# A background pump's credit in a four-layer attention kernel: income 0.6 and cap 1.0 changed to 0.56 and 0.6

## The chip, the cores and the metric

One core of one Trainium2 chip runs the whole program. The metric is the device time of one execution in microseconds. A set of runs is given by its median, and two kernels are compared by the ratio of their mean times in the same rounds on the same chip, with a 95% interval. Faster or slower needs 2%.

## The reference

Four attention layers in a row on x (2048 rows of 640), each with a layer norm before and a residual after, 32 heads of 20. Layers 0 and 2 (weights A) look back over a window of 256 keys; layers 1 and 3 (weights B) look at all 2048.

```python
x = x + _A_ref(_layernorm(x), A_wqkv, A_wo)   # windowed, W = 256
x = x + _B_ref(_layernorm(x), B_wqkv, B_wo)   # full
x = x + _A_ref(_layernorm(x), A_wqkv, A_wo)
x = x + _B_ref(_layernorm(x), B_wqkv, B_wo)
# each: qkv = x @ wqkv; p = softmax(mask(q k^T * 20**-0.5)); (p v) @ wo
```

## The kernel before

The kernel is recorded as one stream of **tiles**. A tile is three PSUM banks of scores (two, in every second tile of layer 0 and of the start of layer 1), one exponential on ScalarE over all of them, and later the products with v. Between the scores of one tile and those of the next, the recording loop puts **background work**: projections of q, k and v (groups of five matmuls into one bank, which VectorE then empties), output projections (groups of eight), transposes, and the small matmuls of a unit's "tail" (the division by the softmax sum). Each task is a generator. `pump` lets tasks run as long as there is credit; `choose` picks the task; a matmul of 512 columns costs 0.22, one of 320 columns 0.14.

```python
    def choose(blocked, limit=1 << 30):
        if state["held"] is not None:
            return state["held"]
        for t in tails:
            if t.wake <= state["tick"]:
                return t
        if not blocked:
            for t in todo:
                if t.wake <= state["tick"] and (t.need <= limit or t.holds):
                    return t
        return None

    def pump(credit):
        state["credit"] = min(state["credit"] + credit, 1.0)
        while True:
            t = choose(state["credit"] <= 0.0)
            if t is None:
                break
            state["credit"] -= advance(t)
```

```python
    def project(wt, n, xt, dst):
        mb = yield from take_m()
        pq = ps[:, mb, :]
        for dc in range(KD):
            nc.tensor.matmul(
                pq, lhsT=wt[:, n, dc, :], rhs=xt[:, dc, :],
                start=(dc == 0), stop=(dc == KD - 1),
            )
            if dc < KD - 1:
                yield ("hold", 0.22)
        evac(dst(), pq)
        drop_m(mb)
        yield ("pe", 0.22)
```

A full layer's unit (one head group, one chunk of 512 queries) starts only when its projections are stored in device memory and read back. `require` forces missing tasks out at once, whatever the credit; `load_ahead` issues the loads of the next units as soon as what they need is recorded.

```python
    def require(what):
        n = 0
        while what not in ready:
            n += 1
            assert n < 100000, what
            t = choose(False, state["unit"] if n < 400 else 1 << 30)
            if t is None:
                state["tick"] += 1
                continue
            state["credit"] = max(state["credit"] - advance(t), -1.0)
# ...
    def load_ahead():

        for u in full:
            if id(u) not in loaded:
                ensure_loaded(u, False)
                return
```

The loop, cut:

```python
        for t in range(len(tiles) + 8):
            # ... start_unit(u) for units that begin here: require(...) and the loads
                sp = ps[:, 0:3, :] if t % 2 == 0 else ps[:, 3:6, :]
                for n in range(2):
                    for i, (u, j, m, b0, subs, first, last, end) in enumerate(cur):
                        for kc, q0, qn, col in subs[n : n + 1]:
                            nc.tensor.matmul(
                                sp[:, i, col * P : (col + qn) * P],
                                lhsT=u.k(kc, j), rhs=u.q(j, q0, qn), start=True, stop=True,
                            )
            # ... the exponential into pt (L804)
                load_ahead()
                pump(1.2 if cur[0][0].l == 0 else 0.6)
            else:
                pump(2.0)
            # ... masks, and the products with v of the tile two or three before (L843)
```

From layer 1's second part on, one single bank (number 6) serves all background work.

The softmax here doesn't subtract the row's maximum and nothing guards it: scores larger than these inputs give would overflow.

Of the kernel before, what the change touches and what calls it, by code (L numbers as in the profile page):

```python
# [31 lines left out]
def kernel(  # L32
# [119 lines left out]
    state = {"tick": 0, "held": None, "credit": 0.0, "early": True, "act": True, "unit": 0}  # L152
# [15 lines left out]
    def push(name, gen, need):  # L168
        insort(todo, Task(name, gen, need))
# [7 lines left out]
    def advance(task):  # L177
        state["running"] = task
        try:
            kind, n = next(task.gen)  # L180
        except StopIteration:
            drop(task)
            state["held"] = None
            return 0.0
        state["held"] = task if kind == "hold" else None
        if kind == "wait":
            task.wake = state["tick"] + n
            return 0.0
        return n
# [10 lines that stand above are left out]
                    return t  # L200
        return None

    def pump(credit):
        state["credit"] = min(state["credit"] + credit, 1.0)
        while True:
            t = choose(state["credit"] <= 0.0)
            if t is None:
                break
            state["credit"] -= advance(t)
# [23 lines left out]
# [10 lines that stand above are left out]
# [261 lines left out]
    def push_layer(l, c):  # L504

        need = [first_use(l, c, g) for g in range(G)]
        push(("ln", l, c), t_ln(l, c), need[0])
        if l == 1:
            push(("v", l, c, 0), t_v(l, c, (0,)), need[0])
            push(("v", l, c, 1), t_v(l, c, (1,)), need[4])  # L510
        else:
            push(("v", l, c), t_v(l, c, (0, 1)), need[0])
        for g in range(G):
            key = ("qk", l, c, g)
            if l % 2:
                push_proj(key, l, 1, g, t_qk_full(key, l, c, g), need[g])
            else:
                push_proj(
                    key, l, 0, g, t_qk_window(key, l, c, g), need[g], first=(l == 0 and c == 0)
                )  # L520
# [206 lines left out]
    def t_stats0(c):  # L727
        for i in range(4):
            stats(0, c, i)
            yield ("pe", 0.1)  # L730
        ready.add(("x", 0, c))
# [12 lines left out]
    with tc.manual_schedule():  # L744
        push("stats", t_stats0(0), 0)
        push_layer(0, 0)
        require(("xnT", 0, 0))
        other_constants()
        require(("qk", 0, 0, 0))

        def narrow(u):
            return u.l == 0 or (u.l, u.part) == (1, "a")

        banks = [b for u in units for b in u.banks]
        tiles = []
        n = 0
        while n < len(banks):
            size = 2 if len(tiles) % 2 and narrow(banks[n][0]) else 3
            tiles.append(banks[n : n + size])
            n += size  # L760

        started = set()
        pts = deque()
        pushed = set()
        for t in range(len(tiles) + 8):
            state["tick"] += 1
            n_b = 0
            if t < len(tiles):
                cur = tiles[t]
                n_b = len(cur)  # L770
                for b in cur:
                    u = b[0]
                    if id(u) not in started:
                        started.add(id(u))
                        if u.l == 0 and u.g == 0 and u.c + 1 < NC and u.c not in pushed:
                            pushed.add(u.c)
                            push(("stats", u.c + 1), t_stats0(u.c + 1), index[0, u.c + 1, 0, None])
                            push_layer(0, u.c + 1)
                            if u.c == 0:
                                push("prep_b", t_prep_b(), index[0, 1, G - 1, None])  # L780
                        state["unit"] = index[u.l, u.c, u.g, u.part]
                        state["act"] = u.l == 0
                        if state["early"] and not narrow(u):
                            end_early()
                        start_unit(u)
# [8 lines that stand above are left out]
                for b in cur:  # L794
                    if b[-1]:
                        s_emitted(b[0])
                pt = ptp.tile([P, 3, C], BF16, name="pt", tag="pt")
                i = 0
                while i < n_b:
                    b0 = cur[i][3]  # L800
                    k = i
                    while k < n_b and cur[k][3] == b0:
                        k += 1
                    nc.scalar.activation(  # L804
                        out=pt[:, i:k, b0 * P :], in_=sp[:, i:k, b0 * P :],
                        func=ACT.Exp, scale=SCALE,
                    )
                    i = k
                for i, b in enumerate(cur):
                    pts.append((t, pt, i, b))  # L810
                load_ahead()
                pump(1.2 if cur[0][0].l == 0 else 0.6)
            else:
                pump(2.0)

            if 0 < t <= len(tiles):
                cur_, pt_ = masked
                i = 0
                while i < len(cur_):
                    m, b0 = cur_[i][2:4]  # L820
                    k = i
                    while k < len(cur_) and cur_[k][2] == m:
                        k += 1
                    if m is not None:
                        mv_ = masks[:, m, b0 * P :].unsqueeze(1).to_broadcast(
                            (P, k - i, C - b0 * P)
                        )
                        nc.vector.tensor_tensor(  # L828
                            out=pt_[:, i:k, b0 * P :], in0=pt_[:, i:k, b0 * P :], in1=mv_,
                            op=ALU.mult,  # L830
                        )
                    i = k
            if n_b:
                masked = (cur, pt)

            if len(pts) >= 4 and pts[3][0] <= t - (3 if pts[0][3][0].windowed else 2):
                group = [pts.popleft() for _ in range(4)]
                u, subs, end = group[0][3][0], group[0][3][4], group[3][3][7]
                first, last = group[0][3][5:7]
                for n, (kc, q0, qn, col) in enumerate(subs):  # L840
                    for _, pt, i, b in group:
                        j = b[1]
                        nc.tensor.matmul(  # L843
                            op[32 * j : 32 * j + VW, q0 * P : (q0 + qn) * P],
                            lhsT=u.v(kc, j), rhs=pt[:, i, col * P : (col + qn) * P],
                            start=(first and n == 0), stop=(last and n == len(subs) - 1),
                            skip_group_check=u.windowed,
                        )
                if end:
                    pv_emitted(u)  # L850
                    finish_unit(u)
        while tails or todo:
            state["tick"] += 1
            pump(5.0)


# [28 lines left out]
```

## Time and profile before

| | before |
|---|---|
| time, four runs of the first comparison | 2526.7 us median (2521.3 to 2529.6) |
| span of the profiled run | 2512.9 us |
| ScalarE (ACT) busy | 2264.0 us, 90% |
| ACT's waits for score matmuls, 376 to 1760 us | 114.1 us in 113 waits |
| the same from 1760 us on | 5.1 us in 7 waits |

In the page's strip of 40 slices each digit is the busy share in tenths; in a group line "busy, mean ns" is followed by the engine's idle time just before these instructions and by what ended it; in a wait line stand the total, the number and the longest. The lines themselves stand in the prediction. The profiled execution is a fast one: it was timed at 2514.7 us, below all four of the first comparison, so the trace of an ordinary execution looks some 7 us or more worse against it than the times are. What is to be learnt from the lines is that ACT is the bound, and that only the stage of layers 1, 2 and the start of 3 still has idle time on it worth winning.

### The profile page before, as it was taken

Reading aid. Unit: us, or ns where it says so; the run is one execution under the profiler, and the core shown is the slowest. Engines: PE = TensorE matmul, PEld = TensorE weight load, DVE = VectorE, ACT = ScalarE, POOL = GpSimd, SP = SyncE. Lnnn points to the kernel's source line nnn. Section 1 sums busy time; section 2 is a strip of 40 time slices with the busy share of each in tenths; the row PEclk is TensorE's granted clock in tenths of the full one; section 3 lists DMA queues with packets and bytes.
Section 4 is the critical chain, followed back from the end, with each engine's and each line's share of the span. In section 5 each row is a group of like instructions: output and inputs, shape, how many; then the busy total and the mean of one; then the engine's idle time right before and its main releaser. Section 6 shows DMA issues by size and latency. Waiting matters only on the chain.

```text
span 2512.9 us, 37403 instructions
## 1 busy us (share of the span) xinstructions
PE 2049.3 (82%) x15313; PEld 730.0 (29%) x15424; DVE 851.9 (34%) x1925; ACT 2264.0 (90%) x1831; POOL 48.2 (2%) x113
## 2 busy tenths in 40 slices
PE   6788987887878898778987888888877787778777
PEld 3334432222322233223332233223322222222222
DVE  6787842321324333434343433643300010001001
ACT  6778866899998999899999988899999999999995
POOL 2000000000000000000000000000000000000000
PEclk9999998885866689757896589869755565556555
DMA  4212133332210133011221023204211010011100
GB/s 162 72 59 64 51 107 91 111 107 68 67 45 26 34 95 110 30 32 41 90 93 39 8 75 104 66 14 122 79 36 48 32 43 32 33 46 46 32 17 11
DMA packets 92892, 153.03 MB, mean 61 GB/s; under 512 B 8880, under 2 KB 59056, under 8 KB 92720
## 3 DMA queue, kind: packets, MB, share of 16 engines
q1 hardware_dynamic: 92720, 150.64, 19.4%
q8 instruction: 120, 1.97, 0.3%
q14 instruction: 52, 0.43, 0.1%
HBM read 120.46 MB, written 30.15 MB: 60 GB/s over the span
## 4 chain that ended last, share of the span: by engine, by line
ACT 47%; PE 28%; issue 13%; DVE 9%; DMA 2%; SPq 0%; ACTq 0%; POOL 0%; DVEq 0%
ACT pt L804 46%; PE ps L318 9%; PE ps L790 6%; PE ps L843 4%; PE ps L482 4%; PE ps L405 4%; DVE pt L828 3%; DMA wqk<-wqk_d 1%; DVE oT L668 1%; PE ps L369 1%; DVE st L266 1%; DMA qt<-q_d 1%; DVE on L718 1%; DVE qa L266 1%; DVE x_sb L490 1%
## 5 line engine op out<-in xcount | busy, mean ns | idle before, releaser
L804 ACT ACTIVATE pt<-ps 128x1536 bf16<-128x1536 f32 (+1 forms) x1688 | 2198.2, 1537 | 184.6 <-PE ps L790 167.3
L790 PE MATMUL ps<-qt,kt 32*128 32x512 bf16 x4096 | 713.9, 504 | 302.4 <-ACT pt L804 268.8
L843 PE MATMUL ps<-pt,vt 128*21 128x512 bf16 x4096 | 533.8, 507 | 6.0 <-DVE oT L668 3.6
L790 PEld LDWEIGHTS <-kt 32*128 32x128 bf16 x4096 | 204.2, 95 | 771.5 <-issue 738.3
L318 PE MATMUL ps<-xnT,wqk 128*128 128x512 bf16 x1169 | 345.0, 413 | 34.8 <-DMA wqk<-wqk_d 7.8
L828 DVE TENSOR_TENSOR pt<-pt,masks 128x1024 bf16<-128x1024 bf16 (+5 forms) x403 | 239.7, 624 | 215.6 <-ACT pt L804 215.3
L668 DVE CAST oT<-ps 128x512 bf16<-128x512 f32 x117 | 80.2, 685 | 505.5 <-PE ps L843 505.1
L843 PEld LDWEIGHTS <-vt 128*21 128x21 bf16 x4096 | 106.0, 91 | 330.5 <-issue 326.3
L482 PE MATMUL ps<-wop,on 128*128 128x320 bf16 x1024 | 179.2, 323 | 9.9 <-DVE x_sb L490 5.1
L318 PEld LDWEIGHTS <-wqk 128*128 128x128 bf16 x1280 | 115.6, 102 | 190.1 <-issue 99.2
L790 PE MATMUL ps<-qa,ka 32*128 32x384 bf16 (+2 forms) x1408 | 132.5, 318 | 31.3 <-ACT pt L804 28.9
L266 DVE CAST st<-ps 128x512 bf16<-128x512 f32 x119 | 82.3, 691 | 208.5 <-PE ps L318 208.1
L490 DVE TENSOR_TENSOR x_sb<-x_sb,ps 128x320 bf16<-128x320 bf16 x128 | 61.9, 484 | 186.3 <-PE ps L482 183.8
L482 PEld LDWEIGHTS <-on 128*128 128x128 bf16 x1024 | 98.0, 104 | 78.1 <-issue 37.5
L405 PE MATMUL ps<-wv,xnT 128*128 128x320 bf16 x640 | 114.2, 317 | 6.8 <-DVE vs L266 2.4
L718 DVE TENSOR_TENSOR on<-oT,ps 128x512 bf16<-128x512 bf16 x128 | 87.5, 683 | 87.4 <-PE ps L714 87.0
L843 PE MATMUL ps<-pt,va 128*21 128x384 bf16 (+2 forms) x1408 | 87.3, 315 | 18.6 <-DVE oT L668 17.9
L695 DVE RECIPROCAL rz<-ps 128x16 f32<-128x16 f32 x128 | 32.7, 256 | 154.0 <-PE ps L690 142.4
L405 PEld LDWEIGHTS <-xnT 128*128 128x128 bf16 x640 | 58.5, 101 | 50.3 <-issue 29.4
L790 PEld LDWEIGHTS <-ka 32*128 32x128 bf16 x1408 | 39.4, 96 | 115.7 <-issue 110.0
L714 PE MATMUL ps<-rT,spread 32*128 32x128 bf16 x512 | 62.9, 256 | 3.2 <-DVE rT L707 2.3
L369 PE MATMUL ps<-ident,xn 128*128 128x128 bf16 x320 | 36.3, 261 | 26.2 <-DVE xn L360 23.3
(50 smaller groups left out, 645.7 us busy)
## 6 DMA issues: line engine op xcount, KB each, us to landing
wqk<-wqk_d SPq DMA_DIRECT2D x120, 320.0 KB
kt<-k_d SPq DMA_DIRECT2D x53, 512.0 KB
vt<-v_d SPq DMA_DIRECT2D x53, 336.0 KB
qt<-q_d SPq DMA_DIRECT2D x75, 128.0 KB
k_d<-st SPq DMA_DIRECT2D x64, 128.0 KB
q_d<-st SPq DMA_DIRECT2D x64, 128.0 KB
v_d<-vs SPq DMA_DIRECT2D x16, 336.0 KB
wqk_d<-wqk SPq DMA_DIRECT2D x16, 320.0 KB
```

The costliest lines, as they stand in the source:

```text
L266: nc.vector.tensor_copy(out=out_, in_=in_)
L318: nc.tensor.matmul(pq, lhsT=wt[:, n, dc, :], rhs=xt[:, dc, :], start=(dc == 0), stop=(dc == KD - 1),)
L405: nc.tensor.matmul(pv, lhsT=xt[:, dc, i * P : (i + 1) * P], rhs=wv_sb[l % 2][:, dc, h * HD : (h + 1) * HD], start=(dc == 0), stop=(dc == K ...
L482: nc.tensor.matmul(yp, lhsT=on[:, g, qb * P : (qb + 1) * P], rhs=wop[:, g, i * HD : (i + 1) * HD], start=(g == 0), stop=(g == G - 1),)
L490: nc.vector.tensor_tensor(out=xv, in0=xv, in1=yp, op=ALU.add)
L668: nc.vector.tensor_copy(out=oT[:], in_=op)
L714: nc.tensor.matmul(zb[:, qb * P : (qb + 1) * P], lhsT=spread4[:, qb, :], rhs=rT[:], start=True, stop=True,)
L718: nc.vector.tensor_tensor(out=on[:, g, :], in0=oT[:], in1=zb, op=ALU.mult)
L790: nc.tensor.matmul(sp[:, i, col * P : (col + qn) * P], lhsT=u.k(kc, j), rhs=u.q(j, q0, qn), start=True, stop=True,)
L804: nc.scalar.activation(out=pt[:, i:k, b0 * P :], in_=sp[:, i:k, b0 * P :], func=ACT.Exp, scale=SCALE,)
L828: nc.vector.tensor_tensor(out=pt_[:, i:k, b0 * P :], in0=pt_[:, i:k, b0 * P :], in1=mv_, op=ALU.mult,)
L843: nc.tensor.matmul(op[32 * j : 32 * j + VW, q0 * P : (q0 + qn) * P], lhsT=u.v(kc, j), rhs=pt[:, i, col * P : (col + qn) * P], start=(first ...
```

## The change

The intent: less background work at a time, two or three matmuls a tile in place of bursts of up to eight, so that the scores of the next tile are not held up. The income per tile falls from 0.6 to 0.56 in layers 1 to 3, and the credit that can be saved up from 1.0 to 0.6. Layer 0 and the end keep their numbers.

```diff
-    def pump(credit):
-        state["credit"] = min(state["credit"] + credit, 1.0)
+    def pump(credit, most):
+        state["credit"] = min(state["credit"] + credit, most)
 ...
-                pump(1.2 if cur[0][0].l == 0 else 0.6)
+                if cur[0][0].l == 0:
+                    pump(1.2, 1.0)
+                else:
+                    pump(0.56, 0.6)
             else:
-                pump(2.0)
+                pump(2.0, 2.0)
 ...
-            pump(5.0)
+            pump(5.0, 5.0)
```

## The prediction

> **What bounds the kernel now.** I read the page first: the busy shares, then the strip of 40 slices.
>
> ```profile
> PE 2049.3 (82%) x15313; PEld 730.0 (29%) x15424; DVE 851.9 (34%) x1925; ACT 2264.0 (90%) x1831; POOL 48.2 (2%) x113
> ...
> ACT  6778866899998999899999988899999999999995
> ...
> PEclk9999998885866689757896589869755565556555
> ```
>
> ScalarE (ACT), which takes the exponential of every score tile, is busy 90% of the span. It is not full in the first six slices (layer 0, where it also empties PSUM for others), nearly full from slice 7 to 28, and full after that. The group view, kept apart by shape, shows what it does, and the wait view of ACT shows what interrupts it, first in the middle of the span (376 to 1760 us), then in the rest:
>
> ```profile
> L804 ACT ACTIVATE pt<-ps 128x1536 bf16<-128x1536 f32 x1509 | 2056.3, 1613 | 136.8 <-PE ps L790 120.6 <-issue 3.0 <-ACT pt L804 2.8
> ```
>
> ```profile
> ACT pt L804 <- PE ps L790: 114.1, 113, 8.1
> ```
>
> ```profile
> ACT pt L804 <- PE ps L790: 5.1, 7, 1.4
> ```
>
> So the change can win only in the middle stage, where ACT waited 114.1 us in 113 waits for the score matmuls of L790, 4.5% of the time. After 1760 us it waits 5.1 us in all. The view by stretches says the same: ACT is busy 1261 of 1384 us, then 722 of 728.
>
> ```profile
> 376.00:1760.00 1384.00, 1146.79 (x8685) 412.05 (x8755) 505.67 (x1086) 1261.14 (x953) 15.34 (x42) 0.78 0.22 67
> 1760.00:2488.00 728.00, 577.86 (x3692) 168.62 (x3690) 76.80 (x201) 722.49 (x538) 0.00 (x0) 0.55 0.12 38
> ```
>
> The first stage (0 to 376 us) is mostly layer 0, whose call of pump keeps its old numbers.
>
> Why does ACT wait? I lined the exponentials of the trace up with the program's tiles. In layers 1 to 3 a background group in every second tile costs nothing: before the 129 tiles n with groups in n-3 and n-1 and none in n-2, ACT waited 2.1 us in all. Ordinary waits come where a group follows the small matmuls of a unit's tail (55 cases, 36.5 us) and in the tile after that (31 cases, 18.4 us), and where two groups stand in neighbouring tiles without a tail before them (24 cases, 6.7 us). The five longest waits are of another kind, 8.1, 6.2, 5.6, 5.0 and 4.5 us: four of them stand where a unit begins whose inputs are not ready, so that the recording loop forces the missing groups out at once (its function require) or the unit's loads have only just been issued. The timeline of one:
>
> ```profile
> 1565.90 1.25 PE L318 MATMUL ps<-xnT,wqk 128*128 128x512 bf16 x5 [1.20 <-DMA wqk<-wqk_d]
> 1567.19 0.69 DVE L266 CAST qa<-ps 128x512 bf16<-128x512 f32 x1 [2.09 <-PE ps L318]
> 1567.93 1.24 PE L318 MATMUL ps<-xnT,wqk 128*128 128x512 bf16 x4 [0.78 <-DVE qa L266]
> ...
> 1570.39 2.79 ACT L804 ACTIVATE pt<-ps 128x1536 bf16<-128x1536 f32 x2 [4.96 <-PE ps L790]
> ```
>
> Two forced groups of five matmuls; the second waits for VectorE to empty the single background bank. From the start of one to the start of the next are 1567.93 - 1565.90 = **2.03 us**, and ACT is idle 4.96 us before its next exponential.
>
> **What the Trainium skill says.** "Perfetto Trace Analysis" (section Identifying the Most-Contended Engine) judges ScalarE by occupancy and TensorE not by matmul busy time. The trace agrees: PE is 82% busy but with the clock at half in the last third, where ACT has no gaps. "ScalarE: Activation LUTs" (What ACT_TABLE_LOAD costs) gives an ACTIVATE with immediate scale and bias 186 ns + 0.833 ns per column and an overlap of about 93 ns back to back, so for 1536 columns 1.37 us; the timeline has 16 exponentials in 21.80 us, 1.36 each. The tile's pace on ACT is thus already the engine's own. "PSUM — Partial Sum Buffer" (Engine vs sequencer instructions) says that matmuls start and complete in program order, so a group recorded before the next scores does delay them. "Perfetto Trace Analysis" (Optimizing Tensor Performance, Matmuls) wants independent groups to rotate through banks, so that emptying one overlaps the next; the forced pair above shows the opposite, 0.78 us of PE waiting for the evacuation.
>
> **The change part by part.** It adds and removes no instruction: 15424 matmuls stand in TensorE's order in both programs. It only alters how the recording loop hands out credit, and only in tiles of layers 1 to 3: income per tile 0.6 becomes 0.56, and what may be saved up falls from 1.0 to 0.6.
>
> (a) The intended part, shorter bursts, does not happen, by my reading. The credit is looked at only for tasks that are not in the middle of a group: choose returns the held task first, whatever the credit, and project, t_v and t_out keep themselves held from the first to the last matmul of a group. So a group that starts, ends in the same tile. The instruction order confirms it. Unbroken runs of one source line, before and after: eight of L482 120 and 120; five of L405 102 and 102; five of L318 245 and 236. No run of two or three appears. Each value of credit above zero still buys a whole group, which costs 1.1; the cap only makes the debt deeper, 0.6 - 1.1 = -0.5 in place of 1.0 - 1.1 = -0.1, and the next tile's income lifts it to 0.06, above zero, so the second group follows at once as before.
>
> (b) The long-run rate falls: 0.6 / 1.1 = 0.545 groups a tile to 0.56 / 1.1 = 0.509, 7% less. Many groups slide one or two tiles back (321 of 1666 tiles differ). I counted the patterns again in the changed program and gave each the mean wait that it had in the trace: neighbouring groups without a tail fall from 24 to 4 (-5.6 us), the tile after tail and group rises from 31 to 34 (+1.8 us), tail and group falls from 55 to 53 (-1.3 us), others give a few us back. The sum of ordinary waits goes from 102.1 to 101.3 us: **-1 us**, nothing.
>
> (c) Slower metering leaves groups over when a unit needs them, and they are forced out. In the order of L318 matmuls, a run of 30 appears where before the longest was 15, and one more run of 15. By tile: where layer 2's last chunk first needs its projections, six groups in place of two (the stall shown above, 4.96 us): 4 x 2.03 = +8.1 us. At the last unit before layer 3, two in place of one (6.18 us now): +2.0 us. At the first unit of the second part of layer 1's first chunk, two in place of none; there PE waits now 4.4 us for loads that can only start when the last group has been stored, so the groups come in front: 2 x 2.03 = +4.1 us. ACT has run dry in all three, so all of it lies on the path. Sum **+14 us**. Groups forced there were taken from elsewhere, which is in (b).
>
> Total: 2523.9 - 1 + 14 = 2537. I take 2535, as a forced group can overlap a load's wait.
>
> **The rivals.** 1: metering works as its title says. If two or three matmuls really stood in each tile, the 114 us would lose what is not forced waits: 114.1 minus 29.4 for the five longest is 85 us, of which half or more might go: 2440 to 2480. For it speaks only the title; against it the order of instructions, which keeps every group whole. 2: the backlog grows, the forced stalls get much longer than counted, for example because the weights of the forced groups aren't loaded (the timeline shows 1.20 us for such a load) or because the store and reload behind them queue up. Three more such waits in the run of 30 would be +4 us; 2550 is the most that I can make of it. 3: the granted clock. In the last third it is 0.5 while PE does only scores and values, and 0.9 to 1.0 where groups come densely. If sparser groups let it fall in the middle stage, a group of five would take up to twice its 1.25 us and ordinary waits would grow. Against it: groups are still in about every second tile where they are dense. If the 7% lower rate acted on all ordinary waits, that would be +-7 us. 4: the delayed groups relieve more than I count, since the deeper debt keeps a group away from tail tiles; at t=161 the order shows tail and group in one tile torn apart. If a quarter of the 55 us of tail waits went, 2523.9 + 14 - 14 = 2524.
>
> **Range and chances.** The kernel's own runs spread from 2521.3 to 2529.6. Rival 4 gives 2524, rivals 2 and 3 up to 2550. With the spread: 2518 to 2552 should hold it 8 times in 10. Faster by over 2% needs under 2473, which only rival 1 gives: 2%. Slower by over 2% needs over 2574, more than twice the forced cost counted: 3%. Within 2%: 95%.
>
> **What the changed kernel's profile would show.** (a) right: ACT waits for L790 in the middle stage still about 110 to 130 us in some 100 to 115 waits, and matmuls of L318 in the timeline still in fives; wrong: 60 us or less. (c) right: one ACT wait of 11 to 15 us near 1570 us where 4.96 us stood, with groups of L318 about 2 us apart before it, and the waits at about 421 and 1497 us longer by 4 and 2 us; wrong: no wait over 9 us after 400 us. (b) right: ACT idle without those stays within 8 us. Granted clock of the middle stage 0.78 within 0.02 (rival 3 if lower). The stage after 1760 us keeps its length of about 728 us. The prediction fails if ordinary waits change by over 20 us either way, which my pattern count does not see.

## The result, and the profile after

The changed kernel takes **2544.9 us** (2541.6 to 2548.2) where the kernel before takes 2526.7: ratio 1.0075, 95% interval 1.0048 to 1.0101. A second set on another occasion gave 1.0087 (1.0065 to 1.0110). A ratio is the mean time of one kernel's runs over that of the other's of the same rounds, so it is not quite the ratio of the medians. It is within 2%, but clear of noise: some 19 to 22 us slower.

The page after, the lines that answer to those of before:

```profile
PE 2071.1 (81%) x15424; PEld 732.8 (29%) x15424; DVE 852.5 (33%) x1925; ACT 2261.2 (89%) x1831; POOL 48.2 (2%) x113
...
ACT  5788866788989999999999989799999999999996
...
PEclk9899988787775589856997589969765565556555
```

Busy times are nearly those of before (PE's extra 22 us are for the most part matmul records of L318 that the first trace lacked: x15313 against x15424 in all). The time went into ACT's idle time. Its group line and its waits in the middle stage, 376 to 1780 us here because the stage ends later, then in the rest:

```profile
L804 ACT ACTIVATE pt<-ps 128x1536 bf16<-128x1536 f32 x1509 | 2052.9, 1612 | 171.8 <-PE ps L790 147.2 <-issue 13.6 <-DVE stats L338 2.5
```

```profile
ACT pt L804 <- PE ps L790: 130.3, 96, 11.9
ACT pt L804 <- issue: 13.6, 5, 7.7
```

```profile
ACT pt L804 <- PE ps L790: 8.3, 8, 1.4
```

The exponentials cost the same (1612 ns against 1613); the idle time before them rose from 136.8 to 171.8 us. There are fewer waits, 96 against 113, and longer ones.

In the stretch 376 to 1780 us the granted clock is 0.79:

```profile
376.00:1780.00 1404.00, 1154.35 (x8742) 412.44 (x8741) 505.20 (x1086) 1255.66 (x953) 16.91 (x45) 0.79 0.22 65
```

The two profiles differ by 33 us, the timed runs by 19 to 22, as the trace before is of a fast execution. Lining the exponentials up with the tiles of the program splits it: start-up +1.4 us, layer 0 +6.0 us (same code in both), **tiles 154 to 1143 +25.9 us** (1454.1 to 1480.0), the rest -0.2 us, the end +0.1 us. Layer 0 lasted between 312 and 318 us in the traces of kernels that don't differ there, and in a second trace of the changed kernel itself (e5) tiles 154 to 1143 lasted 10.3 us longer than in the first. So lengths of this stage from one trace each are good to some 10 us.

The timeline of the longest wait, at tile 989 (columns: start, length, engine, line, what it does, count, idle before and its releaser); weight loads of TensorE and some lines are left out:

```profile
1588.01 1.24 PE L318 MATMUL ps<-xnT,wqk 128*128 128x512 bf16 x5 [0.26 <-DVE va L266]
...
1590.03 1.24 PE L318 MATMUL ps<-xnT,wqk 128*128 128x512 bf16 x5 [0.78 <-DVE st L266]
...
1592.05 1.24 PE L318 MATMUL ps<-xnT,wqk 128*128 128x512 bf16 x5 [0.78 <-DVE st L266]
...
1598.11 1.24 PE L318 MATMUL ps<-xnT,wqk 128*128 128x512 bf16 x5 [0.78 <-DVE qa L266]
...
1600.56 2.79 ACT L804 ACTIVATE pt<-ps 128x1536 bf16<-128x1536 f32 x2 [11.87 <-PE ps L790]
```

Six whole groups stand one after the other, 2.02 us apart, five of them after 0.78 us of waiting for VectorE to empty the one bank, and ACT is idle 11.87 us (4.96 before).

What the prediction had not seen are three new waits of 7.9, 6.6 and 5.0 us at tiles 248, 269 and 291, where no matmul is forced. The first of them:

```profile
494.74 2.30 PE L318 MATMUL ps<-xnT,wqk 128*128 128x512 bf16 x5
...
497.80 0.32 SPq L464 DMA_DIRECT2D q_d<-st  x1
498.21 0.38 SPq L599 DMA_DIRECT2D vt<-v_d  x1
498.69 0.40 SPq L606 DMA_DIRECT2D kt<-k_d  x1
499.14 0.42 SPq L608 DMA_DIRECT2D qt<-q_d  x1
503.54 0.61 PE L790 MATMUL ps<-qt,kt 32*128 32x512 bf16 x2 [5.85 <-DMA qt<-q_d]
...
504.25 2.79 ACT L804 ACTIVATE pt<-ps 128x1536 bf16<-128x1536 f32 x2 [7.88 <-PE ps L790]
```

The unit's last group is recorded in the tile before the unit starts. Its store, the unit's three loads and the first score matmul follow each other, and TensorE waits 5.85 us for the load of q (5.69 and 5.56 us at the other two tiles). In the kernel before, the same loads were issued four tiles ahead, and the wait at tile 248 was 0.0 us.

### The profile page after: what moved, and what is told of

It reads as the page before. It is cut to its first block, busy times and chain, and to the rows that moved or that the text cites.

```text
span 2546.1 us, 37515 instructions
## 1 busy us (share of the span) xinstructions
PE 2071.1 (81%) x15424; PEld 732.8 (29%) x15424; DVE 852.5 (33%) x1925; ACT 2261.2 (89%) x1831; POOL 48.2 (2%) x113
## 4 chain that ended last, share of the span: by engine, by line
ACT 49%; PE 26%; issue 14%; DVE 8%; DMA 2%; SPq 1%; POOL 0%; ACTq 0%; DVEq 0%
ACT pt L804 48%; PE ps L318 9%; PE ps L790 6%; PE ps L846 4%; PE ps L482 3%; PE ps L405 3%; DVE pt L831 2%; DMA qt<-q_d 1%; PE ps L369 1%; DVE oT L668 1%; DVE st L266 1%; DMA wqk<-wqk_d 1%; DVE on L718 1%; DVE qa L266 0%; DVE ka L266 0%
## 5 line engine op out<-in xcount | busy, mean ns | idle before, releaser
L804 ACT ACTIVATE pt<-ps 128x1536 bf16<-128x1536 f32 (+1 forms) x1688 | 2195.2, 1536 | 215.2 <-PE ps L790 188.8
L318 PE MATMUL ps<-xnT,wqk 128*128 128x512 bf16 x1280 | 370.7, 427 | 24.9 <-DVE st L266 7.1
L318 PEld LDWEIGHTS <-wqk 128*128 128x128 bf16 x1280 | 117.8, 104 | 201.0 <-issue 116.6
```

The source lines that it names most:

```text
L318: nc.tensor.matmul(pq, lhsT=wt[:, n, dc, :], rhs=xt[:, dc, :], start=(dc == 0), stop=(dc == KD - 1),)
L804: nc.scalar.activation(out=pt[:, i:k, b0 * P :], in_=sp[:, i:k, b0 * P :], func=ACT.Exp, scale=SCALE,)
```

## The experiments

**Theory A**: the change loses time only where it makes a unit's last group late, either forced out at the unit's start or with its load exposed. **B**: the lower cap does harm by where it puts groups. **C**: the lower cap is a gain that the lower income hides. **D**: the loss is spread over all groups.

### e1_cap_only

```diff
-                    pump(0.56, 0.6)
+                    pump(0.6, 0.6)
```

> Income 0.6 as before, cap 0.6 as after. Theory A (late groups: time is lost only where a unit's last group comes so late that it is forced out or its load is exposed): the order forces three groups where before forces two (tile 989), and nothing else gets late (the load at tile 248 stands 3 tiles ahead, 4 before), so +2 us, at most +4, over before. Theory B (the cap itself does the harm, for instance as it moves groups next to tails): most of the +18 us, so +12 or more. Theory C (the lower cap is a gain that the lower income hides): under before by 4 us or more.

Measured: 2517.0 us, ratio to before 0.9985 (0.9972 to 0.9998). The cap by itself costs nothing: B falls. A's +2 us isn't there either, the interval is 0.5 to 7.1 us under before. The gain is within the 4 us below which C was not to be read.

### e2_rate_only

```diff
-                    pump(0.56, 0.6)
+                    pump(0.56, 1.0)
```

> Income 0.56 as after, cap 1.0 as before. A: four groups forced at tile 989 (two before), two at 211 (none), two at 941 (one), load at tile 248 one tile ahead (4 before), at 269 three ahead (6): about +4, +3, +3, +5 and +2 us, so +13 to +18 us over before, and the waits at 269 and 291 much shorter than after's 6.6 and 5.0 us. B: at most +6 us. C: more than after's +18.

Measured: 2517.7 us, ratio 0.9993 (0.9974 to 1.0012). I was wrong on the sum: not 13 to 18 us slower, but the same. The waits came nearly as expected, see the table below (211: +3.1, 941: +1.8, 989: +5.7, 248: +4.1, 269: +0.4 us), but tiles 185 and 188 gave 3.3 us back and all waits outside the table another 3 us. In the trace tiles 154 to 1143 are 6.3 us longer, which the timing does not show and two traces of one kernel can differ by. So neither number does it alone; A's count of costs was right and its neglect of what is given back was not.

### e3_one_stage

```diff
-                    pump(0.56, 0.6)
+                    pump(*((0.6, 1.0) if (cur[0][0].l, cur[0][0].c) == (1, 0) else (0.56, 0.6)))
```

> After, but with before's income and cap in the tiles of layer 1's first chunk alone (tiles 154 to 333). A: the waits of 7.9, 6.6 and 5.0 us at tiles 248, 269 and 291 go (load 4 and more tiles ahead again) and the one at 211 is back at about 4.5 us, those at 941 (8.9 us) and 989 (11.9 us) stay: 15 to 23 us less than after in the trace, so only about 0 to +8 us over before. If the loss is spread over all groups (theory D) the stage holds about a quarter of them: at least +12 us over before.

Measured: 2521.1 us, ratio 1.0005 (0.9990 to 1.0021). Undoing the change in 180 of the 1657 tiles takes the loss away, 0.9% by the second set of the changed kernel. D falls. The forced waits at 941 and 989 are all still there (8.6 and 11.9 us). They are 9.3 us longer than before, but the interval of the time ends at +5.3 us: what gives the rest back is not known. (The trace is of the slowest of this run's five executions, 2531.1 us.)

The waits of ACT (us) in the traces at the tiles in question, and in brackets how many tiles ahead of the unit's start its loads were issued:

| tile | before | cap only | rate only | one stage | after |
|---|---|---|---|---|---|
| 185 and 188 | 7.7 | 7.7 | 4.4 | 6.2 | 3.7 |
| 211 | 4.5 | 4.6 | 7.6 | 4.5 | 7.7 |
| 216 | 8.1 | 8.1 | 8.0 | 8.5 | 7.3 |
| 248 | 0.0 (4) | 0.5 (3) | 4.1 (1) | 0.0 (4) | **7.9 (0)** |
| 269 | 0.0 (6) | 0.0 (over 6) | 0.4 (3) | 0.0 (6) | **6.6 (0)** |
| 291 | 0.7 (over 6) | 0.0 (over 6) | 0.0 (6) | 0.7 (over 6) | **5.0 (0)** |
| 941 | 6.2 | 7.4 | 8.0 | 8.6 | 8.9 |
| 989 | 5.0 | 6.2 | 10.7 | 11.9 | 11.9 |
| sum | 32.2 | 34.5 | 43.2 | 40.4 | 59.0 |
| tiles 154 to 1143, length | 1454.1 | 1451.4 | 1460.4 | 1464.4 | 1480.0 |

Between four tiles ahead and none lies a whole load: 0.0, 0.4 to 0.5, 4.1, and 5.0 to 7.9 us. Four tiles are 4 x 1.36 = 5.4 us, and from the issue of the first load to the first matmul that used the last one the timeline above has 503.54 - 498.21 = 5.33 us (5.21 and 5.17 at tiles 269 and 291). This is why the two halves of the change together cost more than their sum: each moves the loads some tiles closer, and the cost is nothing until the slack is gone.

### e4_income_066

```diff
-                    pump(0.56, 0.6)
+                    pump(0.66, 1.0)
```

> The opposite direction: income 0.66, cap 1.0. The order forces no group in layers 1 to 3, and loads are late only at tiles 153, 216, 221 and 941. A: the waits of before at 211, 216 and 989 (4.5, 8.1, 5.0 us) go or halve, neighbouring groups (44 tiles against 24, 0.3 us each) cost about 6 us: 5 to 14 us under before. Rival E (denser groups delay the exponentials more than forced ones do): +3 us or more over before.

Measured: 2513.1 us, ratio 0.9970 (0.9957 to 0.9982), 8 us under before, as A has it. Of the eight waits of the table only the one at 941 is left above 3 us (4.5 us); ordinary waits (here and below those under 4 us in layers 1 to 3) rise from 102 to 119 us.

### e5_after_again

No edit: the changed kernel.

> The changed kernel itself once more, on the chip and in the rounds of the three runs below, as the first four runs showed that the stage before the change's own (layer 0, same code) ends up to 6 us apart from run to run. Theory A: +14 to +22 us over before, and in the trace the waits at tiles 211, 248, 269, 291, 941 and 989 (7.7, 7.9, 6.6, 5.0, 8.9, 11.9 us in the first profile) within 1.5 us of that. If the first +18 was mostly a property of that set of runs: under +8 us and those waits different.

Measured: 2543.7 us, ratio 1.0087. The waits are 7.7, 7.5, 7.2, 5.1, 9.0 and 11.9 us, each within 0.6 us of the first profile. The loss and its places repeat. The length of the stage does not: it is 10.3 us longer than in the first trace, with ordinary waits of 114.6 us in place of 104.7. This trace is of the slowest of six executions, 2553.3 us.

### e6_income_080

```diff
-                    pump(0.56, 0.6)
+                    pump(0.8, 1.0)
```

> Groups kept whole, income 0.8, cap 1.0. The order forces no group in layers 1 to 3, every load but the one at tile 153 is at least 3 tiles ahead. A: no wait over 4.5 us at 211, 216, 941 or 989; ordinary waits (102 us before, 119 us with income 0.66) 115 to 135 us; together -12 to +6 us against before. Rival E (density costs more than it saves): +10 us or more.

Measured: 2536.0 us, ratio 1.0052 (1.0036 to 1.0069): 13 us slower, outside of what A had. The late waits are gone as expected, but ordinary waits are 135 us: 140 tiles follow three tiles with a group each, and ACT waited 41.8 us before them (68 tiles and 13.2 us before). Half of what the stage loses in the trace is not idle time; e11 below shows what it is. Rival E holds from here on: past an income of about 0.66 the density costs more than lateness saved.

### e7_split_080

```diff
-        if state["held"] is not None:
+        if state["held"] is not None and not blocked:
             return state["held"]
 ...
-                    pump(0.56, 0.6)
+                    pump(0.8, 1.0)
```

> Really metered: the same income 0.8 and cap 1.0 as the last run, but a group in progress is also stopped when the credit is used up (one condition in choose). No group is forced, loads are at least 4 tiles ahead; no tile has more than one whole group's worth, and out-projections of eight are split. Theory F (ordinary waits come from the length of a burst in one tile): ordinary waits fall to 50 to 85 us, so 20 to 50 us under before. Rival G (they come from the total of TensorE's work where a unit's tail and a group meet, at a low granted clock, and a group once split only spreads over two tiles): within 12 us of the run with income 0.8 and whole groups.

Measured: 2595.0 us, ratio 1.0290 (1.0267 to 1.0313). This run does not test what it was to test. `choose` serves layer 0 too, and there groups were now split as well; layer 0 takes 364.8 us in the trace where e6 takes 315.6 (tiles 154 to 1143: 1477.4 and 1468.8). The first 376 us of the two, busy time by engine, e6 and then e7 (columns: length; PE, PEld, DVE, ACT, POOL busy; clock, DMA):

```profile
0.00:376.00 376.00, 309.26 (x2846) 140.79 (x2884) 263.04 (x626) 273.97 (x336) 32.98 (x71) 0.95 0.27 85
```

```profile
0.00:376.00 376.00, 282.04 (x2530) 122.43 (x2563) 243.04 (x582) 242.59 (x303) 29.31 (x67) 0.92 0.20 66
```

### e8_split_056

```diff
-        if state["held"] is not None:
+        if state["held"] is not None and not blocked:
             return state["held"]
```

(with 0.56 and 0.6 as in the changed kernel)

> What the change's title says, taken at its word: income 0.56 and cap 0.6 as after, and groups really stopped when the credit is used up, so never more than three 512-column matmuls a tile from the pump. The order then forces 226 matmuls in 16 tiles (66 in 5 tiles in after), and eleven units have their loads at most 1 tile ahead. A: forced groups cost 2 us per five, 226 / 5 = 45 groups, 90 us, less the 20 us of after's, and late loads add some 15 to 30 us; ordinary waits fall by up to 60 us: +20 to +90 us over before. The title's theory (short bursts win by themselves): under before.

Measured: 2697.0 us, ratio 1.0694 (1.0664 to 1.0725). It has the same flaw, layer 0 takes 368.4 us. Tiles 154 to 1143 alone take 1583.9 us, 130 more than before, which is also more than A's 90. ACT's waits there (397 to 1980 us in this trace):

```profile
ACT pt L804 <- PE ps L790: 240.0, 147, 19.9
```

In layers 1 to 3, waits under 4 us sum to 89.4 us, not to the 102 of before: short bursts do help a little. The longer ones sum to 165 us. In the order of instructions 263 of 339 groups are cut, nearly all into two parts. A cut group keeps the only bank until its last part, nothing else can start, and the backlog is forced out; that this is why the backlog grows is read from the code, not tested with more banks. Of the 175 us that this kernel loses, layer 0 has 56; the other 119 us are what the intent, taken at its word, costs with a single background bank and an income of 0.56.

### e9_split_080_later

```diff
-        if state["held"] is not None:
+        if state["held"] is not None and not (blocked and state["split"]):
 ...
                         state["act"] = u.l == 0
+                        state["split"] = u.l > 0
 ...
-                    pump(0.56, 0.6)
+                    pump(0.8, 1.0)
```

> The two split runs changed layer 0 as well, which I had not intended: choose is shared, and layer 0 became 51 us longer in their traces. This one splits groups in layers 1 to 3 alone, income 0.8, cap 1.0, to be compared with the run of income 0.8 and whole groups (+0.5% over before). Layer 0 is back at 312 to 318 us. Theory F (the length of a burst makes the ordinary waits): under before by 10 us or more. Theory G (it doesn't): as the trace of the first split run has it, middle stage 5 to 15 us longer than with whole groups at 0.8, so +15 to +30 us over before.

Measured: 2539.6 us, ratio 1.0075 (1.0057 to 1.0094). Layer 0 is back at 315.8 us. With groups split, tiles 154 to 1143 take 1472.5 us, with whole groups at the same income 1468.8, and ordinary waits are 134.3 us against 135.1: no gain, so theory F, the intent's own, falls for the groups that are cut here. The order of instructions shows that these are 135 of 331, and hardly those that matter most: of the 38 groups that follow a unit's tail directly only 3 are cut, as the credit has filled up to 1.0 by then.

For groups after a tail e8 is the test, where all 44 are cut. ACT waited 19.7 us after their first parts and 12.3 us after the later ones (forced groups and waits of 4 us and more left out), and in the kernel before 30.5 us after 43 whole ones. Part of the wait has moved to the next tile; the sum is no less. After the other groups it waited 31 us in e8 (246 groups) and 52 us before (283), so there cutting can save something. In e9 it saved little: after the other groups ACT waited 82 us against 87 with whole ones (e6), and after those that follow a tail 39 against 30, though nearly all of these are whole in both.

### e10_warm_one and e11_warm_two

What then makes the ordinary waits? In the trace before, the groups of the middle stage fall into two kinds. In 52 of them the matmuls follow each other in about 0.5 us (512 columns) or 0.25 us (320), in 260 in half of that. After the 52 slow ones ACT waited 74 us in the next two tiles, after the 260 fast ones 40 us (a wait can count twice). So far this is a coincidence of two things in one trace. These two runs put spare matmuls, whose results nobody reads, into quiet tiles, to keep TensorE's clock up:

```diff
+                    n0 = Task.steps
-                    pump(0.56, 0.6)
+                    pump(0.6, 1.0)
+                    if Task.steps == n0 and 154 <= t < 1144 and mfree[6][0] <= state["tick"]:
+                        for _ in range(1):        # e11: 2
+                            nc.tensor.matmul(
+                                ps[:, 6, :], lhsT=ident[:], rhs=masks[:, 0, :],
+                                start=True, stop=True,
+                            )
```

(`Task.steps` counts the steps of background tasks.)

> Before, with its own income and cap and all groups where they were, plus one spare 128x128 by 512 matmul (result never read) in 415 of the tiles 154 to 1143 that have no other background work. Theory H: ordinary waits come from the first group after a quiet stretch, whose matmuls run at half clock: in before's trace the 52 groups with matmuls about 0.5 us (512 columns) or 0.25 us (320) apart are followed by 74 us of waits, 1.4 us each, the 260 at full clock by 40 us, 0.15 us each. If the spare matmul keeps the clock up, fewer than 35 cold groups and 10 to 40 us under before. Rival I: the spare matmul itself comes at the low clock and takes 0.43 us of a tile's 1.36 us where TensorE has 0.14 to spare: +20 us or more, with as many cold groups.

> The same with two spare matmuls in those 415 tiles. H: fewer cold groups than with one, under 20, and 20 to 60 us under before. I: at half clock two take 0.86 us, so each such tile overruns by about 0.7 us: +50 us or more over before.

Measured: 2557.3 us, ratio 1.0145 (1.0123 to 1.0166) with one, 2549.1 us, ratio 1.0123 (1.0097 to 1.0149) with two. H's times are wrong in both. I's time is right for one spare matmul (37 us over before, it had 20 or more) and too high for two (31 us, it had 50 or more); the slow groups, which it left as they were, got fewer. The middle stage of before stands in the prediction with a granted clock of 0.78; with two spare matmuls it is

```profile
376.00:1760.00 1384.00, 1199.70 (x9281) 439.73 (x9419) 498.07 (x1073) 1255.65 (x940) 16.88 (x45) 0.93 0.22 65
```

in the view by stretches, and in ACT's wait view:

```profile
ACT pt L806 <- PE ps L792: 118.9, 186, 8.0
```

The clock rises to 0.93 and the slow groups fall from 52 (74 us) to 43 (65 us) with one and 27 (38 us) with two. So far H is right in direction (it had under 35 and under 20). But the number of ACT's waits rises from 113 to 186. Where groups stand in every second tile, the spare ones fill the tile between: before those 129 tiles ACT waited 2.1 us in all, with one spare matmul 15.2, with two 25.1. And each interruption costs more than the wait: an exponential with a gap after it takes its whole 1.45 us, one in an unbroken row 1.36 us, as the next starts before it has ended. Over tiles 154 to 1143 of the traces ACT's gaps grow by 11.0 us with two spare matmuls, and what the exponentials take beside them by 14.6 us; with one, by 18.9 and 14.3 us.

### e12_warm_quiet

```diff
+                    n0 = Task.steps
-                    pump(0.56, 0.6)
+                    pump(0.66, 1.0)
+                    Task.quiet = 0 if Task.steps != n0 else Task.quiet + 1
+                    if Task.quiet >= 2 and 154 <= t < 1144 and mfree[6][0] <= state["tick"]:
+                        for _ in range(2):
+                            nc.tensor.matmul(  # as above
```

> The two best signs together: income 0.66 and cap 1.0, groups whole, and two spare matmuls only from the second quiet tile of a stretch on (not between groups that stand in every second tile, where the spare ones cost 25 us of waits in the last run against 2 us before). H: against the run of income 0.66 alone (0.3% under before) the wait at the first group of a windowed stretch falls from 1.3 us in 11 tiles to about 0.2, after tails from 0.8 to 0.5, and nothing is added where groups alternate: 10 to 25 us under before. I: the exponentials are delayed by the spare ones in long quiet stretches: same as before or slower.

Measured: **2507.8 us** (2500.1 to 2511.7), ratio to before 0.9937 (0.9916 to 0.9959): 16 us under before. It beats both kernels, though by less than 2%. About half of that, 8 us, is what income 0.66 gave alone (e4); the rest goes to the spare matmuls, though the two were not run in the same rounds. The same windowed tile (634) with income 0.66 alone, and then with the spare matmuls of L822:

```profile
1032.09 0.61 PE L790 MATMUL ps<-qa,ka 32*128 32x384 bf16 x6 [0.73 <-ACT pt L804]
...
1032.64 0.61 PE L318 MATMUL ps<-xnT,wqk 128*128 128x512 bf16 x1
1033.47 1.48 PE L318 MATMUL ps<-xnT,wqk 128*128 128x512 bf16 x3 [0.22 <-issue]
1034.88 0.61 PE L846 MATMUL ps<-pt,va 128*21 128x128 bf16 x8
...
1036.14 1.45 ACT L804 ACTIVATE pt<-ps 128x1536 bf16<-128x1536 f32 x1 [1.41 <-PE ps L790]
```

```profile
1027.18 6.92 ACT L806 ACTIVATE pt<-ps 128x1536 bf16<-128x1536 f32 x5
...
1029.11 0.60 PE L822 MATMUL ps<-masks,ident 128*128 128x512 bf16 x2
...
1030.12 0.40 PE L792 MATMUL ps<-qa,ka 32*128 32x384 bf16 x6 [0.41 <-ACT pt L806]
...
1030.45 1.25 PE L320 MATMUL ps<-xnT,wqk 128*128 128x512 bf16 x5
```

Without them the group's start to the first product with v is 1034.88 - 1032.64 = 2.24 us and ACT waits 1.41 us; with them the five matmuls take 1.25 us and ACT runs through. The eleven tiles of this kind (windowed, a group after two quiet tiles) lost 14.5 us with income 0.66 alone and 1.7 us here. The waits after tails did not get shorter, 36.9 us in 50 tiles against 39.4.

## Why the prediction was right or wrong

- **The bound** held. ACT's exponentials took the same time, and the whole difference of the traces after layer 0 is ACT's idle time: 131.4 us before, 160.1 after in layers 1 to 3. The 1.37 us of an exponential in the prediction is an estimate from the figures of "ScalarE: Activation LUTs"; the trace has 1.36.
- **(a) groups stay whole**: right. Six groups of five stand in the timeline, and the order of instructions had already said so. The waits in the middle stage are 130 us in 96 (with the five "issue" ones 144 us in 101), not 60 or less. That the intended effect would not have helped after a unit's tail, and elsewhere only at the price of a backlog, is what e8 and e9 add.
- **(b) ordinary waits -1 us**: right within the noise, which is 10 us here. Waits under 4 us went from 102.0 to 104.7 us, in the repetition to 114.6.
- **(c) forced groups +14 us**: the mechanism and its three places are right. At tile 989 +6.9 for +8.1 predicted, at 941 +2.7 for +2.0, at 211 +3.2 for +4.1: together +12.8. Groups follow each other in 2.02 us, predicted 2.03. That these waits cost as much time is not shown: e2 keeps 10.6 us of them and e3 9.3, and neither is slower than before by more than 3.0 and 5.3 us at the interval's end.
- **What failed is the sum of (c)**: it counted units whose groups are forced, and left out units whose groups come just in time and whose loads do not. Those are tiles 248, 269 and 291, 19.5 us after and 0.7 before. Rival 2 had the words for it (store and reload behind the groups queue up) and sized it at "the most that I can make of it" 2550, without asking how many tiles ahead each load stood. The table above shows the count that was missing: loads 4, 6 and over 6 tiles ahead became 0, 0 and 0. Against it stand 4.0 us given back at tiles 185 and 188. The predicted 2535 is 10 us under the measured 2545. The range holds it because rivals 2 and 3 had stretched it to 2550; no term of the sum stood for the loads.
- **Rival 1** (2440 to 2480): wrong, as said. **Rival 3**: the granted clock of the middle stage is 0.79 against 0.78; no change. **Rival 4** (relief at tail tiles): not seen, 36.4 us in 53 tiles for 36.5 in 55.
- Of the Trainium skill's four places, the one on rotating banks mattered most: five of the six forced groups wait 0.78 us each for the one bank. That more banks would mend it was not tried, as no bank is free while two sets of three hold scores.

Still open: why the times of e2 and e3 show nothing of the forced waits that their traces keep, and what the waits after tails, some 37 us, consist of.

## What to carry to other kernels

Before trusting a throttle, look where it is read: one that is looked at only between whole groups changes when groups come, not how long they are. A small cut in the rate of background work costs nothing while every consumer has slack and a whole load's latency once a consumer has none, so count, for each consumer, how many tiles ahead its input is issued. And before making bursts shorter, find out which bursts hurt: some of them here meet TensorE at half clock after a quiet stretch (eleven tiles, where two spare matmuls ahead took the waits from 14.5 to 1.7 us). Spare matmuls in well-chosen tiles and a little more income were worth 16 us; spare matmuls in every quiet tile cost 31 to 37.

## What the Trainium skill lacked or had wrong

- "TensorE: Matmul & The Clock Gate" (The HAM clock gate, What's actually happening) has the array at half clock by default and at full clock after a busy window of about 3.4 us. The traces agree on the two speeds (five matmuls of 512 columns take 2.30 us at tile 248 and 1.24 us at tile 989); the length of the window was not measured. What it lacks, beyond short pauses that make the clock swing, is that a TensorE which is never idle for long can stay near half clock: in the stretch below, of the kernel before, PE is busy 48.2 of 62.8 us, idle for 0.73 us at most at a time, with matmuls that use 32 rows or 21 columns of the array each, and the granted clock is 0.53. Two spare matmuls of full size in quiet tiles raised it from 0.78 to 0.93 over the middle stage.

```profile
1821.20:1884.00 62.80, 48.22 (x305) 13.08 (x302) 5.54 (x14) 62.80 (x48) 0.00 (x0) 0.53 0.10 35
```

- "Perfetto Trace Analysis" (Identifying Performance Opportunities) sends the reader to the gaps of the contended engine and doesn't say what a gap takes beside itself. "ScalarE: Activation LUTs" (What ACT_TABLE_LOAD costs) has the overlap of about 93 ns between exponentials in a row, and each gap loses it: 1.45 us for one of 1536 columns before a gap, 1.36 us in a row of 16. Many short waits are therefore dearer than their sum: with two spare matmuls 14.6 us beside 11.0 us of gaps.
- No page says how far ahead a load must be issued in a loop of this kind. Here three loads of 128 to 512 KB issued together needed 5.2 to 5.3 us to the first matmul that used the last (three cases), four tiles of 1.36 us.
